# k^T v of a pair of heads as two 64-column products per chunk, and four transfers instead of seven for q, k and v of the pair

## The chip, the cores and the metric

One core of one Trainium2 chip. The metric is the device time of the kernel in microseconds (us); lower is better. A ratio is the mean time of one kernel's fast runs over that of the other's fast runs of the same rounds; it is not quite the ratio of the medians that are quoted beside it. The experiments ran on three chips, each beside the kernel before in the same rounds, so versions of different rounds are best compared by their ratios.

## The reference

An attention without softmax, then an RMS norm, then a feed-forward block:

```
kv  = einsum('bhsd,bhse->bhde', k, v)      # batch 8, heads 8, seq 576, head_dim 64
out = einsum('bhsd,bhde->bhse', q, kv)
x   = out / sqrt(mean(out*out, -1) + 1e-6) * g_norm   # then (B*S, H*D) = (4608, 512)
h   = x @ w_in                             # 512 -> 2048
y   = (h * erf(softplus(h))) @ w_out       # 2048 -> 512
```

All operands reach the kernel as fp32; the two weight matrices come in 64 bits and are turned into fp32 on the chip.

## The kernel before

Heads are worked on in 32 pairs (T is the batch, p the pair in it). The 576 positions of a head are 6 chunks (C) of 96 rows (KR). k and v of a pair lie interleaved in SBUF, chunk by chunk the 64 columns of head 0 and of head 1, so that one product of 128 columns per chunk gives both heads' k^T v, as the two diagonal 64x64 blocks of a 128x128 result.

```python
def load_pair(i):
    ...
    t = q_sb[T, p] = pool.tile([P, J + 1, 2, D], FP32, ...)
    for i in range(2):
        nc.sync.dma_start(out=t[:, 0:J, i, :], in_=q[T, 2 * p + i, 0:G, :]...)
    nc.sync.dma_start(out=t[0:R, J], in_=q[T, 2 * p : 2 * p + 2, G:S, :]...)      # the last 64 rows
    for name, got, src in (("k", k_sb, k), ("v", v_sb, v)):
        t = got[T, p] = pool.tile([KR, C, 2, D], FP32, ...)
        for i in range(2):
            nc.sync.dma_start(out=t[:, :, i, :], in_=src[T, 2 * p + i].rearrange("(r c) d -> r c d", c=C))

load_pair(0); load_pair(1); load_pair(2)
... g_col: two transfers of 256 B, needed by VectorE ahead of its first copy out of PSUM
... four weight blocks of 512 KB (w_raw), then pair 3 once pair 0's buffers are free

def products():                                       # cut
    for c in range(C):
        nc.tensor.matmul(kv_ps[:, 0:P], lhsT=ks[:, c], rhs=vs[:, c], start=(c == 0), stop=(c == C - 1))
    nc.tensor.transpose(kv_ps[:, q_tail], qs[0:R, J], ident[0:R, 0:R])            # 64 rows
    for i in range(2):
        s = slice(i * D, i * D + D)
        nc.vector.tensor_copy(out=bd[s, s], in_=kv_ps[s, s])                      # the two blocks
    ...
    for j in range(J):
        nc.tensor.transpose(qt_ps[:, j * P : j * P + P], qs[:, j], ident)
def apply():                                          # bd_kv times q: "L274" and "L275"
    ...
def norm():                                           # mean of squares by a product, then ACT and DVE
    ...
```

The first batch (T = 0) is done at the start, the second beside the first quarter of the feed-forward block, the six others (24 pairs) inside the TensorE-bound rest.

## Time and profile before

| | before |
|---|---|
| median time | 1121.2 us (3 runs, 1119.7 to 1121.7) |
| TensorE busy, share of the span | 94% |
| k^T v products (L258) | 384 records, 52.2 us busy |
| transfers for q, k, v | 7 per pair, 3,456 packets of 256 B |

A TensorE record overlaps its successors (a 128-column product has a record of 275 ns and starts every 111 ns when others follow), so busy time is no cost; what counts is the distance from one start to the next. What the transfers cost as a whole the page says in its part on queues:

```profile
DMA packets 134488, 55.30 MB, mean 49 GB/s; under 512 B 115488, under 2 KB 131872, under 8 KB 134432
...
q1 hardware_dynamic: 134432, 54.55, 18.5%
```

Nearly all packets are small, but the transfer engines are busy for 18.5% of the span only: they can matter in a stretch, not on the whole.

### The profile page before, as it was taken

What the parts mean: (1) busy time and instruction counts of PE and PEld (TensorE: products, weight loads), DVE (VectorE), ACT (ScalarE), POOL (GpSimd) and SP (SyncE); (2) the same over time, 40 slices, a digit from 0 to 9 for tenths busy, and PEclk for the clock granted to TensorE, in tenths of its full rate; (3) what the DMA queues carried; (4) which work ended last, traced back from release to release, by engine and by line L of the source; (5) the groups of instructions that cost most, each with busy time, mean ns of one, the idle gap of its engine ahead of it and who ended that gap; (6) DMA issues with size and microseconds to landing.
All of it is one profiled execution on the core that took longest, in us unless ns stands there. A gap on an engine that the chain in (4) does not pass through costs nothing.

```text
span 1121.4 us, 11926 instructions
## 1 busy us (share of the span) xinstructions
PE 1050.5 (94%) x4584; PEld 836.8 (75%) x4584; DVE 713.6 (64%) x1180; ACT 486.5 (43%) x652; POOL 100.7 (9%) x71
## 2 busy tenths in 40 slices
PE   6576887899999999999999999999999999999996
PEld 4232443458888888888888888888888888888885
DVE  1678788637776656675567556755675567666545
ACT  1444444544444444444444444444444455442222
POOL 0257556200000000000000000000000000000000
PEclk9886988999999999999999999999999999999999
DMA  8345434102111211121112111211120001001001
GB/s 206 97 123 146 125 94 127 32 10 61 32 32 32 70 33 32 32 70 32 32 32 70 32 32 32 70 32 33 32 70 1 1 1 38 1 1 38 1 1 38
DMA packets 134488, 55.30 MB, mean 49 GB/s; under 512 B 115488, under 2 KB 131872, under 8 KB 134432
## 3 DMA queue, kind: packets, MB, share of 16 engines
q1 hardware_dynamic: 134432, 54.55, 18.5%
q8 instruction: 36, 0.59, 0.2%
q14 instruction: 20, 0.16, 0.0%
HBM read 45.09 MB, written 9.44 MB: 49 GB/s over the span
## 4 chain that ended last, share of the span: by engine, by line
PE 82%; DVE 10%; ACT 4%; issue 2%; SPq 1%; POOL 0%; DMA 0%; DVEq 0%; ACTq 0%; POOLq 0%
PE p_ps L483 68%; PE kv_ps L258 3%; PE o_ps L336 3%; PE se_ps L275 2%; DVE w_m L207 2%; PE ms_ps L287 2%; DVE e L431 1%; PE qt_ps L269 1%; DVE w_e L203 1%; DVE w_e L182 1%; PE h_ps L409 1%; DVE w_e L174 1%; SPq L121 1%; DVE w_m L186 1%; ACT w_e L185 1%
## 5 line engine op out<-in xcount | busy, mean ns | idle before, releaser
L359 ACT ACTIVATE s_sb<-h_sb 128x512 f32<-128x512 f32 x144 | 89.9, 630 | 337.5 <-DVE h_sb L431 337.0
L431 DVE TENSOR_TENSOR h_sb<-h_sb,p_ps 128x512 f32<-128x512 f32 x224 | 148.2, 684 | 116.0 <-PE p_ps L483 114.8
L483 PE MATMUL p_ps<-w_out_sb,h_sb 128*128 128x256 f32 x768 | 176.4, 380 | 1.0 <-DVE h_sb L585 1.0
L483 PEld LDWEIGHTS p_ps<-w_out_sb,h_sb 128*128 128x128 f32 x768 | 145.8, 190 | 21.5 <-DVE h_sb L585 1.8
L483 PE MATMUL p_ps<-x_sums,a_sums 128*128 128x256 f32 x512 | 122.8, 384 | 4.9 <-issue 4.9
L431 DVE TENSOR_TENSOR e<-e,p_ps 128x512 f32<-128x512 f32 x120 | 80.8, 684 | 71.6 <-PE p_ps L483 71.0
L483 PE MATMUL p_ps<-x_sums,w_in_sb 128*128 128x256 f32 x512 | 121.0, 379 | 0.0
L483 PEld LDWEIGHTS p_ps<-x_sums,a_sums 128*128 128x128 f32 x512 | 98.4, 192 | 28.9 <-issue 16.2
L483 PE MATMUL p_ps<-w_sums,s_sb 128*128 128x256 f32 x512 | 116.3, 380 | 0.0
L483 PEld LDWEIGHTS p_ps<-x_sums,w_in_sb 128*128 128x128 f32 x512 | 97.4, 190 | 25.1 <-issue 13.4
L483 PEld LDWEIGHTS p_ps<-w_sums,s_sb 128*128 128x128 f32 x512 | 95.2, 190 | 15.9 <-DVE h_sb L431 4.0
L483 PE MATMUL p_ps<-xT,w_in_sb 128*128 128x256 f32 x448 | 101.3, 379 | 0.0
L483 PEld LDWEIGHTS p_ps<-xT,w_in_sb 128*128 128x128 f32 x448 | 83.3, 190 | 10.3
L98 ACT ACT_TABLE_LOAD x69 | 88.5, 1283 | 1.2
L431 DVE TENSOR_TENSOR h_sb<-h_sb,s_sb 128x512 f32<-128x512 f32 x128 | 82.2, 685 | 5.5 <-ACT s_sb L364 5.5
L296 DVE SCALAR_TENSOR_TENSOR qT<-ms_ps,qT 128x512 f32<-128x512 f32 x36 | 24.9, 692 | 95.5 <-ACT qT L293 95.5
L409 PE MATMUL h_ps<-xT,w_in_sb 128*128 128x512 f32 x128 | 67.2, 672 | 16.4 <-ACT h_sb L417 11.0
L364 ACT ACTIVATE s_sb<-s_sb 128x512 f32<-128x512 f32 x144 | 78.8, 618 | 0.4
L278 ACT ACTIVATE qT<-se_ps 128x512 f32<-128x512 f32 x32 | 19.0, 594 | 115.5 <-PE se_ps L275 115.5
L409 PEld LDWEIGHTS h_ps<-xT,w_in_sb 128*128 128x128 f32 x128 | 27.8, 221 | 53.6 <-issue 32.6
L258 PEld LDWEIGHTS kv_ps<-v_sb,k_sb 96*128 96x128 f32 x384 | 51.8, 206 | 16.4 <-issue 12.8
L185 ACT ACTIVATE w_e<-w_e,exp_col 128x512 int32<-128x512 int32 x32 | 23.1, 722 | 89.5 <-DVE w_e L182 89.5
(76 smaller groups left out, 1374.7 us busy)
## 6 DMA issues: line engine op xcount, KB each, us to landing
k_sb<-in_k_dram SPq DMA_DIRECT2D x64, 144.0 KB, 3.0
v_sb<-in_v_dram SPq DMA_DIRECT2D x64, 144.0 KB, 3.1
q_sb<-in_q_dram SPq DMA_DIRECT2D x64, 128.0 KB, 2.9
w_raw<-in_moe_w_in_dram SPq DMA_DIRECT2D x16, 512.0 KB, 3.7
w_raw<-in_moe_w_out_dram SPq DMA_DIRECT2D x16, 512.0 KB, 3.8
out_dram<-e SPq DMA_DIRECT2D x28, 256.0 KB, 2.1
q_sb<-in_q_dram SPq DMA_DIRECT2D x32, 32.0 KB, 2.5
out_dram<-o_sb SPq DMA_DIRECT2D x4, 256.0 KB, 2.2
```

Of the source, the lines that this page charges most:

```text
L98: nc.scalar.preload_act_table_set("softplus")
L185: nc.scalar.activation(e, e, AF.Identity, scale=float(1 << 23), bias=exp_col)
L207: nc.vector.scalar_tensor_tensor(out=m, in0=lo, scalar=2.0**-52, in1=m, op0=ALU.mult, op1=ALU.add)
L258: nc.tensor.matmul(kv_ps[:, 0:P], lhsT=ks[:, c], rhs=vs[:, c], start=(c == 0), stop=(c == C - 1))
L275: nc.tensor.matmul(o_ps, lhsT=bd, rhs=qT[:, 0:G], start=True, stop=True)
L296: nc.vector.scalar_tensor_tensor(out=u, in0=ms_ps, scalar=EPS, in1=u, op0=ALU.add, op1=ALU.mult)
L336: nc.tensor.matmul(o_ps[j], lhsT=g[:, j * P : j * P + P], rhs=w_out_sb[:, f, :], start=(f == 0), stop=(f == FC - 1),)
L359: nc.scalar.activation(s, h, AF.Softplus)
L364: nc.scalar.activation(s, s, AF.Erf)
L409: nc.tensor.matmul(h_ps, lhsT=w_in_sb[:, c, n * P : n * P + P], rhs=xT[0][:, c, :], start=(c == 0), stop=(c == KC - 1),)
L431: nc.vector.tensor_tensor(out=out_, in0=x, in1=y, op=op)
L483: nc.tensor.matmul(ps[:, i * H : i * H + H], lhsT=a[:, c, i * P : i * P + P], rhs=x[:, c, :], start=(first and c == 0 and (i == 0 or last) ...
```

## The change

Its intent: compute only the two blocks that are used, on the two halves of the array at the same time; and move k and v in runs of 1,536 B instead of 256 B, with four transfers per pair instead of seven. The two go together in one respect: with head-by-head k and v a chunk's 128 columns are no longer one run, and a stationary operand of two runs does not build (the builder asks for one).

```diff
-        for i in range(2):
-            nc.sync.dma_start(
-                out=t[:, 0:J, i, :], in_=q[T, 2 * p + i, 0:G, :].rearrange("(p j) d -> p j d", j=J)
-            )
+        nc.sync.dma_start(
+            out=t[:, 0:J],
+            in_=q[T, 2 * p : 2 * p + 2, 0:G, :].rearrange("h (p j) d -> p j h d", j=J),
+        )
 ...
-            t = got[T, p] = pool.tile([KR, C, 2, D], FP32, name=f"{name}_sb", tag=name, bufs=bufs)
-            for i in range(2):
-                nc.sync.dma_start(
-                    out=t[:, :, i, :], in_=src[T, 2 * p + i].rearrange("(r c) d -> r c d", c=C)
-                )
+            t = got[T, p] = pool.tile([KR, 2, C, D], FP32, name=f"{name}_sb", tag=name, bufs=bufs)
+            nc.sync.dma_start(
+                out=t.rearrange("r h c d -> r h (c d)"),
+                in_=src[T, 2 * p : 2 * p + 2].rearrange("h (r c) d -> r h (c d)", c=C),
+            )
 ...
             for c in range(C):
-                nc.tensor.matmul(
-                    kv_ps[:, 0:P], lhsT=ks[:, c], rhs=vs[:, c], start=(c == 0), stop=(c == C - 1)
-                )
+                for i in range(2):
+                    s = slice(i * D, i * D + D)
+                    nc.tensor.matmul(
+                        kv_ps[s, s],
+                        lhsT=ks[:, i, c],
+                        rhs=vs[:, i, c],
+                        start=(c == 0),
+                        stop=(c == C - 1),
+                    )
```

## The prediction

> **What bounds the kernel now.** I read the page first: the engines' totals and the chain that ended last.
>
> ```profile
> PE 1050.5 (94%) x4584; PEld 836.8 (75%) x4584; DVE 713.6 (64%) x1180; ACT 486.5 (43%) x652; POOL 100.7 (9%) x71
> ...
> PE 82%; DVE 10%; ACT 4%; issue 2%; SPq 1%; POOL 0%; DMA 0%; DVEq 0%; ACTq 0%; POOLq 0%
> PE p_ps L483 68%; PE kv_ps L258 3%; PE o_ps L336 3%; PE se_ps L275 2%; DVE w_m L207 2%; PE ms_ps L287 2%; DVE e L431 1%; PE qt_ps L269 1%; DVE w_e L203 1%; DVE w_e L182 1%; PE h_ps L409 1%; DVE w_e L174 1%; SPq L121 1%; DVE w_m L186 1%; ACT w_e L185 1%
> ```
>
> The chain is TensorE for 82%. The products that the change touches (L258, k^T v) have 3% of it, some 34 us; the issue of the k and v transfers (SPq L121) has 1%. A share is an average, so I asked for engine time by stretch:
>
> ```profile
> 140.00:160.00 20.00, 16.81 (x35) 7.68 (x36) 16.79 (x27) 10.98 (x17) 12.47 (x8) 0.83 0.37 109
> ...
> 300.00:400.00 100.00, 100.00 (x485) 85.79 (x484) 70.81 (x120) 48.65 (x65) 0.00 (x0) 1.00 0.17 43
> ```
>
> (Columns: PE, PEld, DVE, ACT, POOL busy, granted clock, DMA share, GB/s.) From about 186 us to the end PE has no gap: every ns saved or added on PE there moves the end. Between 28 and 186 us the chain lists VectorE's weight conversion (w_e, w_m) and short PE pieces; extra PE time there is mostly beside it. Before that there is a start-up. The chain in order of time begins so:
>
> ```profile
> 14.92 0.63 SPq L131
> 15.60 2.35 DMA g_col<-in_g_norm_dram
> 19.03 0.66 PE kv_ps L274 x2
> 19.69 1.81 PE se_ps L275 x2
> 21.51 2.56 PE kv_ps L258 x12
> ```
>
> Ahead of these lines stand 20 pieces of 0.6 to 0.7 us, all SPq: the start is bound by how many transfers the queue must issue (three pairs at seven each) before g_col, for which VectorE waits at 18.05 us, in order ahead of its first copies out of PSUM. Last, one burst of the products in the PE-bound part (288 products after 200 us, 12 per pair: 24 pairs):
>
> ```profile
> 307.85 1.50 PE L258 MATMUL kv_ps<-v_sb,k_sb 96*128 96x128 f32 x12
> 309.29 0.27 PE L261 MATMUL kv_ps<-ident,q_sb 64*128 64x64 f32 x1
> 309.49 0.66 PE L269 MATMUL qt_ps<-ident,q_sb 128*128 128x128 f32 x4
> ```
>
> One product's record is 275 ns (median of that line after 200 us), so twelve in 1.50 us start every (1.50 - 0.275) / 11 = 111 ns. A pair of heads now takes 12 x 111 = 1.34 us; from the first product to the next kind it is 1.44, so some 0.1 us is lost on going to the 64-row transpose.
>
> **What the Trainium skill says.** "TensorE: Matmul & The Clock Gate", LDWEIGHTS: a load takes its columns at 1.2 GHz, so 107 ns for 128 and 53 for 64. The trace agrees for 128: two loads for L275 start at 290.46 and together record 0.30 us with 190 ns each, so 110 ns apart. The same page, Part 3, The mechanism, says that a load overlaps running products only where the row group differs; the trace differs, as loads of the same 96 rows run wholly beside the products (111 ns a pair of load and product, where each alone needs about 107). "TensorEngine Tiling (Array Packing)", Key Properties: "Changing tiling mode (not just tile) drains the TensorE", and different tiles can load and multiply in parallel. The 0.1 us gap ahead of L261 agrees with the first; nothing in this trace shows column tiles, so the second is open. "DMA: Bandwidth & Descriptors", Specifications, wants at least 512 B per descriptor; this case's 256 B packets cost, over 2 to 16 us, 0.79 x 16 x 14 us for 179 GB/s x 14 us / 256 B = 9,790 packets, 18 ns each, and the 1,024 B ones (19 to 22.5 us, share 1.04 at 363 GB/s) 47 ns: per byte a third less.
>
> **The change part by part.** Products: per chunk, one 128-column product (of which the two off-diagonal 64x64 blocks are thrown away) becomes two of 64x64, on columns 0-63 and 64-127. An fp32 product is two instructions here (192 products, 384 records), so a pair goes from 12 loads and 12 products to 24 and 24, each of half the columns. A 64-column product already in the kernel (L274) starts its successor (0.33 - 0.275) = 55 ns later. Hence three cases for a pair:
> (a) halves run side by side: 24 / 2 x 56 = 0.67 us;
> (b) no overlap between halves, loads still hidden: 24 x 56 = 1.34 us, as now;
> (c) loads no longer hidden: 24 x 110 = 2.6 us.
> To each comes the entry into the column mode: a drain of 0.1 us as ahead of L261, plus an exposed 64-column load of 0.05 to 0.1 us (after L261 the trace shows 200 ns where 110 is the rule). I take 0.17 us. The way out costs nothing new, since a mode change to 64 rows is there already. So per pair -0.50, +0.17 or +1.4 us, and for 24 pairs -12, +4 or +34 us.
>
> Transfers: per pair 7 issues become 4. Issues take 0.67 us each whether they carry 32 or 144 KB (5.53 to 10.23 us is one pair: 4.70), so 2.7 us a pair. Packets: q stays at 1,152 of 256 B; k and v go from 2,304 of 256 B to 384 of 1,536 B (66 ns each on the line through 18 and 47; an estimate). A pair's transfer goes from 3,456 x 18 / 16 = 3.9 us to 1.3 + 1.6 = 2.9 us. After 28 us nobody waits for q, k or v in this trace, so this is worth something only at the start: v of pair 0 is issued at 2.8 instead of 4.9 us and the first product starts near 6.2 instead of 8.21. g_col is issued at 9.5 instead of 15.6 and lands near 12 instead of 18. PE takes 4.24 us for a pair's products and transposes there (8.21 to 12.45, at half rate: 2.90 us for the twelve), so in case (b) pairs 0 and 1 end at 14.7 and the first L274 comes then, not at 19.03: 4.3 us earlier, bound by PE and no longer by g_col. In case (a) the pairs end near 12.3 and g_col and VectorE's copies (1 us) bind at 13: 6 us, and 1.2 us more from pair 2, which is on the chain at 21.51. The chain from 28 to 186 us is VectorE, ScalarE and PE pieces that the change leaves alone, so it moves as a whole; the w_raw transfers are never waited for.
>
> Sums: (a) -12 - 7 = -19, so 1102; (b) +4 - 4 = 0, so 1121; (c) +34 - 2 = +32, so 1153 us.
>
> **Rivals.** First, that the weight loads remain one stream even if the products overlap: 24 loads x 53 ns = 1.3 us, so (b) by another way. For it: in the kernel before, loads are as long as products (PEld in step with PE in the burst), so halving one of the two gains nothing. Against: the skill's statement that tiles load in parallel. Second, that the sequencer can't feed 48 instructions in 0.7 us. Against: each burst follows products of 216 ns, during which the queue can fill. For: the trace shows nothing quicker than 55 ns. It would land between (a) and (b), 1108 to 1115. Third, that the start's gain is hidden again by another wait: the weights' transfers follow at once and slow the issue of pair 3 (q at 18.59 took 2.23 us for two). But pair 3 is needed only at 28 us and moves forward too; I'd lose at most 2 us. Fourth, case (c), for which the quoted sentence on row groups speaks and the trace's hidden loads speak against.
>
> **Range and chances.** I give (a) with its losses about one half, (b) four in ten, (c) or a good part of it under one in ten. The middle of that is 1110 us; it is a mixture with two peaks, so the range must hold both: 1098 to 1125. Over 2% faster means under 1098.8, which asks for (a) without any loss and a dearer start than I count: 0.09. Over 2% slower (1143.6) is (c): 0.06. Within 2%: 0.85.
>
> **What would show it.** The first product near 6.2 us and the first L274 between 13 and 15 us (start). L258 with 768 products and loads, and in the PE-bound part from the first of them to L261 0.85 us (a), 1.5 us (b) or 2.7 us (c), against 1.44; product starts in couples a few ns apart for (a), an even 55 ns for (b), 110 for (c). A gap of 0.1 to 0.2 us ahead of the first product of each burst. 36,864 + 12,288 packets for q, k and v, and issues for them still near 0.65 us; were a merged issue to take twice as long, the start would gain nothing. The prediction is wrong if the burst of 24 takes over 2 us, or if the time from 28 to 186 us changes its length.

## The result, and the profile after

The changed kernel takes 1107.57 us in the median (4 runs, 1106.26 to 1109.02), the one before 1121.45 in the same rounds; the ratio is 0.9877 (0.9856 to 0.9899). It is 1.2% faster: within the 2% that counts as the same, and inside the predicted range.

The totals and the chain of the changed kernel (L261 is now the line of the products, L490 that of the feed-forward's, L282 and L294 those that were L275 and L287):

```profile
PE 1035.1 (93%) x4968; PEld 812.1 (73%) x4968; DVE 713.2 (64%) x1180; ACT 486.6 (44%) x652; POOL 100.8 (9%) x71
...
PE 82%; DVE 10%; ACT 4%; issue 2%; SPq 1%; DMA 0%; POOL 0%; DVEq 0%; ACTq 0%; POOLq 0%
```

TensorE has 384 more products and 15.4 us less busy time; it is the bound as before. One burst of the products in the TensorE-bound part, from the timeline (start, us, engine, line, operation, tiles, shapes, count):

```profile
303.41 0.81 PE L490 MATMUL p_ps<-w_out_sb,s_sb 128*128 128x256 f32 x3
304.15 0.92 PE L261 MATMUL kv_ps<-v_sb,k_sb 96*64 96x64 f32 x24
305.00 0.27 PE L268 MATMUL kv_ps<-ident,q_sb 64*128 64x64 f32 x1
305.21 0.66 PE L276 MATMUL qt_ps<-ident,q_sb 128*128 128x128 f32 x4
```

From the first product to the 64-row transpose it is 0.85 us, where it was 1.44 us, with twice as many product instructions. A window of 0.03 us at the start of the burst shows why: two products, and two weight loads, begin in it.

```profile
304.15 0.28 PE L261 MATMUL kv_ps<-v_sb,k_sb 96*64 96x64 f32 x2
304.15 0.14 PEld L261 LDWEIGHTS kv_ps<-v_sb,k_sb 96*64 96x64 f32 x2 [0.33 <-issue]
```

In the records of the burst the products start in couples 6 to 7 ns apart, one couple every 58 ns (107 ns after the first); the loads start in couples too, every 55 to 58 ns. Ahead of the burst, the last feed-forward product has 309 ns to the first of L261, where it had 215 to L258: 94 ns are lost on the way into this mode. From burst to burst, with the same feed-forward work between them, it is 27.77 us instead of 28.26, so 0.49 us less per pair.

The start, from the chain in order of time:

```profile
9.43 5.45 DMA g_col<-in_g_norm_dram
15.96 0.66 PE kv_ps L281 x2
16.62 1.81 PE se_ps L282 x2
18.43 1.48 PE kv_ps L261 x24
20.21 1.05 PE qt_ps L276 x4
21.58 1.81 PE se_ps L282 x2
23.39 1.72 PE ms_ps L294 x2
```

The issues are over 6 us earlier (9.43 against 15.60), but g_col then takes 5.45 us to land instead of 2.35, and the first product with bd_kv (L281, formerly L274) starts 3.1 us earlier, not 6. The queues:

```profile
DMA packets 71514, 55.33 MB, mean 50 GB/s; under 512 B 40224, under 2 KB 68896, under 8 KB 71456
...
q1 hardware_dynamic: 71456, 54.54, 17.6%
```

Half of the packets are gone, and the share of the engines' time only fell from 18.5 to 17.6%: the large packets are not much cheaper for what they carry. Engine time from 2 to 13 us, before and then after (columns as in the prediction; the last two are DMA share and GB/s):

```profile
2.00:13.00 11.00, 4.44 (x18) 3.76 (x19) 0.00 (x0) 0.51 (x1) 0.00 (x0) 1.00 0.79 180
```

```profile
2.00:13.00 11.00, 4.69 (x55) 3.88 (x55) 0.00 (x0) 0.59 (x1) 0.00 (x0) 1.00 1.04 239
```

Before, the engines moved 180 GB/s in 79% of their time (228 GB/s if they were always busy); now they are full, at 239 / 1.04 = 230 GB/s. The bound of the start moved from the issue of transfers to the transfer engines.

To add the two parts up I compare the two traces at fixed instructions. VectorE's instruction that stood at 38 us is 2.37 us earlier, the one at 204 us 2.39 us earlier: the stretch between keeps its length. The end is 14.16 us earlier. What lies between is not simply 24 times 0.491 us, as TensorE pauses once more after the first of the 24 bursts. The chain of the kernel before:

```profile
212.18 3.46 PE p_ps L483 x16
215.64 4.86 issue
220.50 3.75 PE p_ps L483 x8
```

The chain calls the pause "issue", so the profile shows nothing that was waited for; but in every trace of this case TensorE goes on 0.10 us after a copy of VectorE out of PSUM ends (220.40 us here), and in the changed kernel it goes on at 218.11, which is 2.39 us earlier, just as VectorE is. What the first of the 24 bursts (210 us) saves is lost in this pause, and 23 bursts count. The other part is TensorE's rate: after the pause the granted clock is one half for 6.08 us in the kernel before and for 5.24 us in the changed one, which is worth half of the difference, 0.42 us. So 2.39 + 0.42 + 23 x 0.491 = 14.1.

### The profile page after: what moved, and what is told of

Read it like the earlier page. It is cut to its first block, busy times and chain, and to the rows that moved or that the text cites. A ratio compares the mean times of both kernels' runs of the same rounds, so it can differ in the third digit from the quotient of the medians.

```text
span 1107.2 us, 12541 instructions
## 1 busy us (share of the span) xinstructions
PE 1035.1 (93%) x4968; PEld 812.1 (73%) x4968; DVE 713.2 (64%) x1180; ACT 486.6 (44%) x652; POOL 100.8 (9%) x71
## 3 DMA queue, kind: packets, MB, share of 16 engines
q1 hardware_dynamic: 71456, 54.54, 17.6%
## 4 chain that ended last, share of the span: by engine, by line
PE 82%; DVE 10%; ACT 4%; issue 2%; SPq 1%; DMA 0%; POOL 0%; DVEq 0%; ACTq 0%; POOLq 0%
PE p_ps L490 69%; PE se_ps L282 3%; PE ms_ps L294 3%; PE o_ps L343 3%; DVE w_m L207 2%; PE kv_ps L261 2%; DVE e L438 1%; PE qt_ps L276 1%; DVE w_e L203 1%; DVE w_e L182 1%; PE h_ps L416 1%; DVE w_e L174 1%; DVE w_m L186 1%; ACT w_e L185 1%; DMA g_col<-in_g_norm_dram 0%
## 5 line engine op out<-in xcount | busy, mean ns | idle before, releaser
L490 PE MATMUL p_ps<-w_out_sb,h_sb 128*128 128x256 f32 x768 | 176.4, 379 | 1.0 <-DVE h_sb L592 1.0
L490 PEld LDWEIGHTS p_ps<-w_out_sb,h_sb 128*128 128x128 f32 x768 | 145.7, 190 | 21.6 <-DVE h_sb L592 1.8
L490 PE MATMUL p_ps<-x_sums,a_sums 128*128 128x256 f32 x512 | 122.8, 383 | 4.1 <-issue 4.1
L490 PE MATMUL p_ps<-x_sums,w_in_sb 128*128 128x256 f32 x512 | 121.0, 379 | 0.0
L490 PEld LDWEIGHTS p_ps<-x_sums,a_sums 128*128 128x128 f32 x512 | 98.3, 192 | 28.2 <-issue 14.9
L490 PE MATMUL p_ps<-w_sums,s_sb 128*128 128x256 f32 x512 | 116.3, 380 | 0.0
L490 PEld LDWEIGHTS p_ps<-x_sums,w_in_sb 128*128 128x128 f32 x512 | 97.3, 190 | 25.2 <-issue 13.4
L490 PEld LDWEIGHTS p_ps<-w_sums,s_sb 128*128 128x128 f32 x512 | 95.1, 190 | 16.0 <-DVE h_sb L438 3.1
L490 PE MATMUL p_ps<-xT,w_in_sb 128*128 128x256 f32 x448 | 101.3, 379 | 0.0
L490 PEld LDWEIGHTS p_ps<-xT,w_in_sb 128*128 128x128 f32 x448 | 83.2, 190 | 10.3
L490 PE MATMUL p_ps<-w_out_sb,s_sb 128*128 128x256 f32 x256 | 60.5, 379 | 0.0
```

Source lines behind the costliest of these rows:

```text
L490: nc.tensor.matmul(ps[:, i * H : i * H + H], lhsT=a[:, c, i * P : i * P + P], rhs=x[:, c, :], start=(first and c == 0 and (i == 0 or last) ...
```

## The experiments

**Theory**, as it stood before the runs. The products save 0.49 us on each of the 24 pairs in the TensorE-bound part because a product on columns 0-63 and one on 64-127 run side by side, loads included; the transfers only shorten the start, by 2 to 3 us, since the transfer engines now bind there. **Rivals.** The transfers carry the gain; the narrow products are quicker by themselves, without lying on different halves; the larger packets, not the fewer issues, help the start.

The table gives, for each version, what it measured and three readings of its trace against that of the kernel before: how much earlier VectorE's instruction stands that was at 204 us (the start's gain), the distance of two bursts, and how much earlier the end is. The times are medians.

| version | time, us | ratio (95%) | earlier at 204 us | burst to burst, us | earlier at the end |
|---|---|---|---|---|---|
| before | 1121.45 | | | 28.26 | |
| after | 1107.57 | 0.9877 (0.9856-0.9899) | 2.4 | 27.77 | 14.2 |
| transfers_only (wrong result) | 1115.9 | 0.9958 (0.9936-0.9981) | 6.4 | 28.27 | 7.9 |
| products_only | 1110.77 | 0.9904 (0.9888-0.9921) | 1.5 | 27.77 | 13.3 |
| half_by_half | 1119.05 | 0.9971 (0.9954-0.9989) | 3.9 | 28.29 | 3.6 |
| gcol_early | 1105.27 | 0.9853 (0.9832-0.9874) | 4.9 | 27.77 | 16.4 |
| same_half (one run) | 1120.71 | | 5.8 | 28.47 | 2.5 |
| issues_only | 1120.06 | 0.9971 (0.9954-0.9988) | 2.6 | 28.27 | 2.7 |
| pieces_1024 (one run) | 1108.31 | | 2.8 | 27.77 | 14.9 |
| warm_start | 1106.99 | 0.9860 (0.9846-0.9875) | 4.5 | 27.77 | 16.2 |
| pair3_first | 1102.86 | 0.9835 (0.9822-0.9848) | 8.4 | 27.77 | 20.4 |
| pair3_warm | 1100.89 | 0.9825 (0.9809-0.9841) | 7.3 | 27.77 | 19.2 |
| tail_full | 1103.34 | 0.9840 (0.9826-0.9853) | 5.5 | 27.68 | 19.6 |
| all_of_it | 1098.87 | 0.9804 (0.9785-0.9823) | 10.1 | 27.68 | 23.6 |

The last column is the start's gain, plus 23 times the change of the distance of bursts, plus half of the time by which the stretch at half rate after the pause got shorter: within 0.13 us for same_half and 0.07 us for all others. That stretch lasts 6.1 us in the kernel before, 3.2 us in transfers_only, 3.6 us in same_half and 4.7 to 5.9 us in the rest, so it is worth 1.4 and 1.2 us in those two and up to 0.7 us elsewhere. Why it is short there isn't known. The readings are each from one profiled run, whose start can differ from that of the timed runs.

### transfers_only

The changed transfers and layout, but as much TensorE work as before. The result is wrong: two chunks of one head at a time are multiplied as if they were two heads.

```diff
-            for c in range(C):
-                for i in range(2): ... two 64-column products
+            for n in range(C):
+                i, c = n % 2, 2 * (n // 2)
+                two = (slice(None), i, slice(c, c + 2))
+                nc.tensor.matmul(kv_ps[:, 0:P], lhsT=ks[two], rhs=vs[two], ...)
```

> The changed transfers and layout, but six 128-column products per pair as before (two chunks of one head at a time; the result is wrong on purpose, the count and size of all TensorE work is that of the kernel before). Theory (the products save 0.49 us on each of 24 pairs, the transfers only shorten the start): burst to the next kind of instruction 1.43 us as before, no extra gap ahead of it, first L274-type product near 16 us instead of 19, total 1118 to 1120 us. Rival (most of the 14 us comes from the transfers): 1108 to 1112 us.

Measured: 1115.9 us (6 runs, 1113.5 to 1121.0), bursts 28.27 us apart. TensorE's part is as expected, without any gain per pair. The start gained 6.4 us in the profiled run, more than in the changed kernel with the same transfers, and the median lies below the expected 1118 to 1120. Chain of this run, at the place of the last two lines of the chain shown above:

```profile
20.80 0.91 PE se_ps L282 x2
21.72 0.87 PE ms_ps L294 x2
```

The same products of 512 columns take half the time here: TensorE was at full rate already, while in the changed kernel it ran at half rate until 25 us. And in the changed kernel it fell back later: engine time from 25 to 35 us, the changed kernel first, then this one (the third number from the end is the granted clock).

```profile
25.00:35.00 10.00, 6.12 (x38) 3.60 (x37) 3.94 (x10) 5.36 (x9) 1.50 (x1) 0.69 0.44 101
```

```profile
25.00:35.00 10.00, 3.46 (x8) 1.86 (x9) 7.21 (x16) 3.53 (x6) 1.69 (x2) 0.90 0.25 66
```

So in these traces what the transfers are worth depends on when TensorE is at full rate in the first 40 us; another 1.4 us of this run's 7.9 come from the short stretch at half rate after 220 us. Whether narrow products, which keep it less busy, delay the full rate, or chance does, is not settled: this version's own runs spread over 7.5 us.

### products_only

The old transfers and layout, with the two 64-column products per chunk (`ks[:, c, i]` and `vs[:, c, i]`).

> The old transfers and layout, with the two 64-column products per chunk. Theory: burst 0.85 us plus 0.09 us ahead of it, so 24 x 0.49 = 12 us less; the first product stays at 8.2 us and g_col at 18 us, but pair 2, on the chain at half rate, saves 1.1 us: 1108 to 1110 us. Rival (the transfers matter): 1116 us or more.

Measured: 1110.77 us (5 runs, 1109.9 to 1112.3), bursts 27.77 us apart, burst to transpose 0.85 us; the total lies a little over the expected 1108 to 1110. In ratios, products alone give 0.96%, transfers alone 0.42% (or 0.29%, see half_by_half and issues_only), both 1.23%. The products carry the gain; the rival falls.

### half_by_half

```diff
-            for c in range(C):
-                for i in range(2):
+            for i in range(2):
+                for c in range(C):
```

> The changed kernel with the two loops exchanged: all six chunks of the first half, then all six of the second; same instructions, other order. Theory (two neighbours in the queue run side by side only when they lie on different halves): only one couple at the seam overlaps, 24 x 55 ns, so the burst takes 1.4 to 1.55 us instead of 0.85, and the total is 1107.6 + 24 x 0.6 = 1121 to 1124 us. Rival (the narrow products are quicker by themselves, or the queue reorders them): 0.85 us and 1107.6 us as in the changed kernel.

Measured: 1119.05 us (6 runs, 1116.1 to 1119.6), correct. The burst:

```profile
303.97 1.43 PE L261 MATMUL kv_ps<-v_sb,k_sb 96*64 96x64 f32 x24
305.33 0.27 PE L268 MATMUL kv_ps<-ident,q_sb 64*128 64x64 f32 x1
```

The same 24 instructions need 1.36 us to the transpose instead of 0.85, and the distance of bursts is back to 28.29. So narrowness alone gives nothing: the gain needs neighbours on different halves. It is a little less than the 1.4 to 1.55 expected, and the total 2 to 5 us less. The records show why: the starts are 58 ns apart but for the middle, where the tenth starts 6 ns after the ninth, and two further couples 4 ns apart follow. Three couples overlap, not one, so the expectation was wrong in this detail (the last section says what the records suggest).

### same_half

Both heads' products on the same half: `kv_ps[0:D, s]` as the output of both, and VectorE copies the second block from partitions 0-63 to 64-127 of bd. Only the very first of the twelve products of a pair carries the start flag (`start=(c == 0 and i == 0)`). The two results still alternate.

> The changed kernel with both products of a chunk on the same half of the array (the second head's result goes to other columns of PSUM partitions 0-63), still alternating between the two results. Theory (they overlap because they lie on different halves): no overlap at all, burst of 24 x 55 ns plus the way out, 1.36 to 1.45 us, like half_by_half. Rival (what matters is that neighbours add to different places in PSUM): 0.85 us as in the changed kernel.

Measured: 1120.71 us (one run), correct.

```profile
301.26 1.61 PE L261 MATMUL kv_ps<-v_sb,k_sb 96*64 96x64 f32 x24
302.80 0.27 PE L269 MATMUL kv_ps<-ident,q_sb 64*128 64x64 f32 x1
```

All 24 starts are 58 ns apart (107 after the first), and the burst takes 1.54 us, more than before the change. It is a tenth of a us over what I expected, as I had left out the slow first step and counted 55 ns. The rival, that alternating results are what helps, falls.

### gcol_early

```diff
     load_pair(0)
     load_pair(1)
-    load_pair(2)
     g_col = ...                 # and its two transfers
+    load_pair(2)
```

> The changed kernel with the two small transfers of g_col issued after pair 1 instead of after pair 2. Theory (the start is bound by g_col, which sits behind pair 2's data in the transfer queue and lands at 14.9 us): g_col lands near 11 to 12 us, VectorE no longer waits for it, the first product with bd_kv starts near 14.1 us instead of 15.96, total 1105 to 1106.5 us. Rival (TensorE or the data of pair 1 binds just as late, or the gain is lost again to the half rate of TensorE near 31 us): 1107 to 1108 us.

Measured: 1105.27 us (4 runs, 1104.5 to 1106.8). VectorE has g_col at 11.3 us instead of 15.0, and the first product with bd_kv comes right behind the transposes of pair 1, as expected or a little sooner:

```profile
12.68 1.11 PE L276 MATMUL qt_ps<-ident,q_sb 128*128 128x128 f32 x4
13.59 0.52 PE L281 MATMUL kv_ps<-qT,bd_kv 128*128 128x64 f32 x2
```

So g_col behind pair 2's data was what the start of the changed kernel waited for. In times the gain over the changed kernel is not clear of noise, as the intervals of the two ratios overlap; the traces (4.9 us at 204 us, against 2.4) and the medians point the same way.

### issues_only

The kernel before with one transfer each for q, k and v of a pair, in the interleaved layout with 256 B runs:

```diff
+            nc.sync.dma_start(
+                out=t, in_=src[T, 2 * p : 2 * p + 2].rearrange("h (r c) d -> r c h d", c=C)
+            )
```

> The kernel before with its interleaved layout and 128-column products, but one transfer each for q, k and v of a pair (4 issues per pair instead of 7, every packet still 256 B). Theory (at the start the number of issues bound, and with four issues the transfer engines bind; the larger packets bring little, as a 1,536 B packet takes 96 ns, hardly less per byte than 18 ns for 256 B): a pair's transfers take 3.9 us, so first products between 7.3 and 8 us, g_col near 15 us, start and total as in transfers_only: 1114 to 1118 us. Rival (the packet size carries the gain): first products at 8.2 us or later, g_col at 17 to 18 us, 1120 to 1122 us.

Measured: 1120.06 us (4 runs, 1117.7 to 1120.5). Neither side is right in all: the start came as the theory said (first product at 7.1 us, g_col at 15.7, the first L274 at 16.7 instead of 19.0), the total as the rival said. I had taken the total from transfers_only, whose early full rate this one did not have (its twelve products of pair 2 still took 2.7 us). Its ratio, 0.9971, is the same as that of half_by_half with the large packets, and the interval overlaps that of transfers_only. From 2 to 13 us:

```profile
2.00:13.00 11.00, 5.47 (x23) 4.79 (x24) 0.00 (x0) 0.59 (x1) 0.00 (x0) 1.00 0.92 208
```

208 / 0.92 = 226 GB/s while busy, against 230 with the large packets. A gain from packet size is not shown; what there is of the start's gain goes with the fewer issues.

### pieces_1024

The changed kernel with each k and v transfer cut into chunks 0-3 (1,024 B) and 4-5 (512 B).

> The changed kernel with each k and v transfer of a pair cut in two: chunks 0-3 (1,024 B packets) and 4-5 (512 B packets), so six issues per pair. It measures what a packet costs in the same 96-row transfers. If the 96 ns of the 1,536 B packet come from its size (not a power of two, or over 1,024 B), the 1,024 B packets take 47 ns as those of the weights do, and the 512 B ones some 28. If they come from reading two rows of 96 partitions or from the load on memory at the start, 1,024 B take 60 to 65 ns. The start is no quicker either way (6 x 0.67 = 4.0 us of issues per pair): total 1107 to 1110 us.

Measured: 1108.31 us (one run). In the packet records of the first 24 us the median is 46 ns for 1,024 B and 27 ns for 512 B, so 73 ns for what one packet of 1,536 B did in 95 ns (median of the same stretch of the changed kernel); in means it is 83 against 95. The total is within a microsecond of the changed kernel's, and g_col lands at 14.7 us as there (two issues more per pair stand ahead of it). But the 1,536 B packet is not slow as such: where one pair is loaded alone (278 to 290 us of the changed kernel) its median is 65 ns (its mean 85, as some packets take far longer). More of them are slow when the engines are full, and why that hits them more than two smaller ones stays open.

### warm_start

gcol_early with 20 products of a constant at the start, while TensorE has no data.

```diff
+    warm_ps = ps_h.tile([P, G], FP32, name="warm_ps", tag="h")
+    for _ in range(20):
+        nc.tensor.matmul(warm_ps[:, 0:P], lhsT=mean_w, rhs=mean_w, start=True, stop=True)
```

> gcol_early with 20 products of 128 columns of a constant, whose result nobody reads, ahead of the first real product, while TensorE has nothing to do. Theory (the products at the start run at half rate because TensorE was idle before): the first burst takes 0.85 us instead of 1.48 at 7.8 us, transposes 0.66 instead of 1.11, and the chain through the first three pairs gets 2 to 4 us shorter: 1101.5 to 1104 us. Rival (the pauses between pairs put it back to half rate, or the data of pair 1 and g_col bind just as late): within 1 us of gcol_early, 1104.5 to 1106 us.

Measured: 1106.99 us (4 runs, 1106.1 to 1107.4), outside both expected ranges and no better than gcol_early. The theory's first half held (bursts of 0.85 us from the first pair on), but the time went into waits:

```profile
15.60 0.92 PE L264 MATMUL kv_ps<-v_sb,k_sb 96*64 96x64 f32 x24 [1.98 <-DMA v_sb<-in_v_dram]
...
25.07 1.55 PE L264 MATMUL kv_ps<-v_sb,k_sb 96*64 96x64 f32 x24 [4.15 <-DMA v_sb<-in_v_dram]
```

TensorE was done with pair 2 early and then stood for 4.15 us until pair 3's v landed, behind the 2 MB of weights, and was at half rate again when it came.

### pair3_first

gcol_early with one weight block ahead of pair 3 and the other three behind it.

```diff
-    for _ in range(RAW):
-        w_next("load")
+    w_next("load")
 ...
                         load_pair(3)
+                        for _ in range(RAW - 1):
+                            w_next("load")
```

> gcol_early with only the first of the four weight blocks issued ahead of pair 3's q, k and v, and the other three behind them. Theory (with four issues per pair the start is bound by the transfer engines, and pair 3 stands behind 2 MB of weights that are needed only one per 8 us): pair 3's products start near 20 us instead of 24.4, and the chain at its end is 2 to 4 us ahead: 1101.5 to 1103.5 us. Rival (the half rate of TensorE or VectorE's weight conversion binds by then, so that pair 3 may come late for nothing): 1104.5 to 1106 us.

Measured: 1102.86 us (5 runs, 1101.9 to 1103.2). Pair 3 starts at 20.3 us, and the start's gain grows from 4.9 to 8.4 us in the traces:

```profile
20.27 0.92 PE L261 MATMUL kv_ps<-v_sb,k_sb 96*64 96x64 f32 x24 [1.28 <-DMA v_sb<-in_v_dram]
```

The intervals of the two ratios still overlap at their ends; the traces and the medians (2.4 us) say the same.

### pair3_warm

pair3_first with the 20 products of warm_start.

> pair3_first with the 20 idle products of warm_start. Theory (in warm_start the quick products only made TensorE wait longer for pair 3's data, 4.15 us; with the data there the 1 to 3 us from the full rate show): 1 to 3 us below pair3_first. Rival: TensorE falls back to half rate in the pauses near 30 us whatever came before: within 1 us of pair3_first.

Measured: 1100.89 us (4 runs, 1100.7 to 1104.0), ratio 0.9825 against 0.9835. The difference is within the intervals, and the profiled run, with 1104.03, is the slowest of the four. Not decided.

### tail_full

gcol_early with q's tail loaded as the last 128 rows and transposed with 128 rows instead of 64.

```diff
-            out=t[0:R, J], in_=q[T, 2 * p : 2 * p + 2, G:S, :]...
+            out=t[:, J], in_=q[T, 2 * p : 2 * p + 2, S - P : S, :]...
-            nc.tensor.transpose(kv_ps[:, q_tail], qs[0:R, J], ident[0:R, 0:R])
+            nc.tensor.transpose(kv_ps[:, P : 2 * P], qs[:, J], ident)
```

> gcol_early with the 64-row transpose of q's tail replaced by a 128-row one (the transfer brings the last 128 rows, of which the first 64 are not used), so that each pair has one change of mode less. Theory (each change of mode drains the array, some 0.1 us): from the first product to the first q transpose 1.05 us becomes 0.95, and the 128-row tail transpose takes 0.11 instead of 0.20; 24 pairs give 2 to 3 us, so 1102.5 to 1103.5 us. Rival (the way out of the column mode costs the same into any mode, and only the narrow transpose itself gets dearer): 1105 to 1106 us.

Measured: 1103.34 us (4 runs, 1103.0 to 1103.6), correct; bursts 27.68 us apart instead of 27.77.

```profile
300.61 0.92 PE L261 MATMUL kv_ps<-v_sb,k_sb 96*64 96x64 f32 x24
301.46 0.33 PE L268 MATMUL kv_ps<-ident,q_sb 128*128 128x128 f32 x1
301.62 0.60 PE L276 MATMUL qt_ps<-ident,q_sb 128*128 128x128 f32 x4
```

The way out of the column mode takes 0.85 us from the burst's start as before, so the rival is right in that. But the tail's transpose is followed after 0.165 us instead of 0.203, and the four transposes after it take 0.437 us instead of 0.492 (medians of the 24 pairs): 0.09 us a pair, 2 us in all. One change of mode less and a wider transpose together are worth that; the two are not told apart. As against gcol_early, the intervals of the ratios overlap, and the distance of the bursts is the evidence.

### all_of_it

pair3_warm with tail_full.

> pair3_warm with the 128-row transpose of tail_full: everything that helped, in one kernel. Theory: the gains lie in different stretches (start, and each pair), so they add: 1101 less 2, 1098.5 to 1100.5 us, correct. Rival (they overlap): 1101 us or more.

Measured: 1098.87 us (5 runs, 1097.8 to 1100.6), correct, ratio 0.9804: 2.0% below the kernel before and the lowest median of all; whether it is over 2% is unclear, as the interval reaches from 0.9785 to 0.9823. The gains of the start and of the bursts add: 10.1 us and 23 x 0.584 = 13.4 us make 23.5 of the 23.6 us in the trace.

## Why the prediction was right or wrong

The time, 1107.6, lay 2.4 us from the predicted 1110 and within the range, and the class (within 2%) was the likely one. But 1110 was the middle of two cases, and the kernel is in one of them, (a), for which the prediction's sum was 1102. That the number came so close is luck; the mechanism of (a) was right, and one term of its sum was not.

**The case.** (a), halves side by side, was given one half; it is what happened. The rival of a single stream of weight loads is refuted by the loads that start in couples, and (b) and (c) with it. half_by_half and same_half are what (b) looks like.

**The products' term** of (a) was -0.50 us per pair and -12 us in all; measured are -0.49 and, as only 23 of the 24 pairs count, -11.3. The reading that TensorE has no gap from about 186 us was wrong: it pauses from 215.64 to 220.50 us, and what the pair ahead of this pause saves is lost in it. That the sum still fits is chance, as 0.4 us came from the shorter half rate behind the pause. Parts of the -0.49: 0.85 us to the transpose, as named for (a); 94 ns on the way in instead of the 0.17 us I allowed for, as the longer first step of the burst (107 ns) is counted in the 0.85. Products start in couples every 58 ns, where I had 56.

**The start's term** was mis-sized: -7 us, of which 2.4 remained. The step that failed is that a pair's transfer goes from 3.9 us to 2.9 us, with its 66 ns per packet of 1,536 B. That figure is the median for a pair loaded alone (65 ns; the mean is 85); with the engines full the median was 95 ns from 2 to 13 us. With the means of that stretch, 20 and 98 ns, a pair takes (1,152 x 20 + 384 x 98) / 16 = 3.8 us, so nearly what it took before; for the three pairs ahead of g_col that makes 3 x 0.9 = 2.7 us (an estimate from these means). The first product came at 7.66 us instead of 6.2, and g_col landed at 14.9 instead of 12, in a queue of transfers that I had seen as empty. The L274 came at 15.96; the prediction said between 13 and 15. gcol_early shows that this wait was the bound. The third rival, that another wait hides the start's gain, so came true, but with g_col as the wait, not pair 3, and for more than its 2 us. Pair 2's quicker burst gave 1.1 us, where 1.2 were predicted. Then 1.5 us were lost between 31 and 38 us (3.9 us ahead, then 2.4), where TensorE ran at half rate in the changed kernel and not in the one before (the two 512-column instructions of the product with bd_kv took 1.10 us at 33.43 us before, 2.04 us at 29.53 us after); the prediction had no such term.

**The stretch from 28 to 186 us** was to move as a whole, and a change of its length was named as a sign of being wrong. It did change, by those 1.5 us, all of them before 38 us. From 38 to 204 us it moved as a whole, within 0.1 us, in all versions.

**Issues** near 0.65 us each: they took 0.45 to 0.87 us. That part was right, and it brought the first three pairs' issues to an end when predicted; it was just no longer what bound. (Ahead of g_col stood 21 issues, three pairs at seven, not the 20 that the prediction counts.)

So the total of (a) was 5 us too low, nearly all of it in the start; the middle of the mixture hid that.

## What to carry to other kernels

Where two small products are independent and each fills only half of the array's columns, put them on different halves and let them alternate in the queue: here the pair cost 0.49 us less although the instructions doubled, and with the loops exchanged nothing was left of it. When fewer transfers are issued, ask what binds next: here it was the transfer engines, and then the order of the transfers (a 256-byte vector behind a pair, a pair behind 2 MB of weights) was worth more than their size. A gain in a start-up is safe only as far as the trace shows that TensorE keeps its rate through the new pauses.

## What the Trainium skill lacked or had wrong

- "TensorE: Matmul & The Clock Gate", Part 3, says that weight loads overlap running products only where the row group differs (though a sentence ahead of it also names a background weight buffer). Here loads of the same 96 rows start 6 to 7 ns apart, a couple every 58 ns, beside running products; that the two of a couple lie on different column halves is inferred from same_half, where there are no couples.
- The same part says that products are strict first in, first out, in start and end. In half_by_half, twelve products of one half stand ahead of twelve of the other; the tenth to start follows the ninth by 6 ns, and three couples overlap, while on one half no two started less than 58 ns apart in same_half. The records don't name the half, so it is inferred: the other half's products began with three of the first half's still to come. For this speaks that the next record of the second stream comes 106 ns after its first, as in the first step of every burst (107 ns).
- "TensorEngine Tiling (Array Packing)", Key Properties, says that a change of mode drains the engine and gives no figure. Here the way into the 64-column mode cost 94 ns (309 instead of 215 ns), and one change less per pair, with a wider transpose, gave 0.09 us.
- "DMA: Bandwidth & Descriptors", Specifications, puts the line at 512 B per descriptor. With the engines full, 256 B packets and a mix with 1,536 B ones moved 226 and 230 GB/s of busy time; the 1,536 B packet took 65 ns alone and 95 ns under load, 1,024 and 512 B ones 46 and 27 ns (medians). No page has these figures.
